# Sparse block attention and a gated feed-forward on one core: 64-query blocks against one 128-row tile of keys and summaries

## The chip, the core and the metric

The kernel runs on one core of one Trainium2 chip. The core has a matrix engine (PE, whose weight loads are listed apart as PEld), a vector engine (DVE), a scalar engine (ACT), GpSimd (POOL), and a sync engine (SP) that here only issues DMAs. They run side by side and wait for one another by semaphores. The metric is the device time of one execution in microseconds (us), lower is better. The kernel before takes 266.48 us, the median of three runs (266.11, 266.48, 267.84).

## What is computed

```python
batch, n_heads, seq, head_dim = (4, 8, 768, 64)      # q, k, v, float32
block, window = (32, 16)
k_sum = k.reshape(B, H, nb, block, D).max(axis=3)     # 24 summaries for each head
v_sum = v.reshape(B, H, nb, block, D).mean(axis=3)
scores_l = scale * q @ k^T, kept where |i - j| < window, else -1e9
scores_s = scale * q @ k_sum^T + log(block)
a = softmax(concat[scores_l, scores_s]);  x = a @ concat[v, v_sum]
# then for the 3072 tokens, d_model 512, d_ff 2048
h = x @ w_in
out = (h * clip(h + 3, 0, 6) / 6) @ w_out
```

A query sees 31 neighbouring keys at most and the 24 summaries of its head. Adding log(32) to a summary's score and taking the mean of v is the same as weighting its exponential by 32 in the row sum and taking the sum of v in the numerator; both kernels use this.

## The kernel before

**Units.** There are four batches and four head pairs `p` in each; a pair's two heads lie in partitions 0 to 63 and 64 to 127. Tokens are cut into eight tiles of 384 (`HALF`), two for each batch; tile `t` is batch `t // 2`.

**Attention of a pair.** `Tk` (L264) transposes k on PE, copies it out of PSUM into `kbd`, a block-diagonal tile with 64 keys of both heads in each of 12 steps, and takes the maximum over each 32 keys (`red`) into `kst`. `Tq` (L298) does the same with q into `qT`. `Sl` (L316) multiplies each 64-key block by the 94 queries that can see it (12 matmuls of 94 columns for a pair), takes the exponential on ACT (L324) and multiplies by a 0/1 band mask on DVE (L325). `Ss` (L327) makes the summary scores, for two pairs together: two matmuls of 384 columns for each half. `AV` (L348) makes one pair's half tile: the numerator `num` is one 384-column matmul with the summaries' values (L357) and seven 15- to 94-column matmuls over key blocks (L359); the row sum `den` is four matmuls with tiles of ones (L363, L366, L369 and L370, or L372 and L373). Then ACT takes the logarithm of `den` and the exponential of its negative (L375, L376), and DVE multiplies (L377) into `x`.

**Feed-forward.** `F1(t, ft)` (L382) is four 384-column matmuls (L389), a Relu on ACT (L392) and a combined minimum and product on DVE (L393) into `g`. `F2` (L395) is 512-column matmuls (L402), a copy on ACT (L406) and a store by SP (L408).

**Loads.** All but the stores and one small copy (L259) are issued by POOL, in program order. k and q of batches 0 and 1 are loaded as long runs (`RUN` = 8 rows of one partition) and transposed in 64-column pieces; those of batches 2 and 3 come in 256-byte rows (L111). Values go to the block-diagonal `vall` (L118); batch 0's come as float32 (`vf`, L127), are cast by ACT and DVE (`vcast`), and summed on PE by float32 matmuls (`vsum0`, L252). For batches 1 to 3 a second copy of v (`vr`, L134) is summed on DVE (`vsum`, L231 to L236).

**Order.** The start is written out by hand for PE, ACT and DVE (L151 to L448): attention of the first half of batch 0. After that a planner orders PE, ACT, DVE and SP; POOL stays in program order. The loop at the end runs `work_list` in slots: each entry is 16 slots of one F1 tile, one F2 tile or both, and `at_slot` puts attention steps into slots. The order is F1(0); F1(1) with F2(0); F2(1); F1(2); then F1(3) with F2(2) and so on, four F1 matmuls and three F2 matmuls in turn; last F2(7) alone. PSUM: `ps_h`, `ps_o` and `ps_s` have two buffers each, `ps_n` has one `num` and one `den`. The SBUF pool `gp` has three buffers, for `g` and for `vf`.

Of the kernel before, what the change touches and what calls it, by code (L numbers as in the profile page):

```python
# [16 lines left out]
D = 64  # L17
BLK = 32
KB = 64
HALO = 15  # L20
WIN = KB + 2 * HALO
HALF = 384
NLONG = 2
RUN = 8
PCS = 4
RP = 96
QCUT = 480
# [3 lines left out]
def kernel(  # L31
# [12 lines left out]
    NB = S // BLK  # L44
    NT = S // 128
    NK = S // KB
# [5 lines left out]
    RS = 4 * NB  # L52

    const = ctx.enter_context(tc.tile_pool(name="const", bufs=1))
    ld = ctx.enter_context(tc.tile_pool(name="ld", bufs=4))
    work = ctx.enter_context(tc.tile_pool(name="work", bufs=2))
    xp = ctx.enter_context(tc.tile_pool(name="xp", bufs=4))
# [11 lines left out]
    kbd = [const.tile([128, NK, 128], BF16, tag=f"kbd{p}", name=f"kbd{p}") for p in range(NP)]  # L69
    vall = const.tile([128, NP, NK, 128], BF16, tag="vbd", name="vbd")  # L70
    vbd = [vall[:, p] for p in range(NP)]
    qT = [const.tile([128, S + 2 * HALO + 2], BF16, tag=f"qT{p}", name=f"qT{p}") for p in range(NP)]
    at = [const.tile([128, NK, WIN], BF16, tag=f"at{p}", name=f"at{p}") for p in range(NP)]
    kst = [const.tile([128, RS], BF16, tag=f"kst{p}", name=f"kst{p}") for p in range(NP)]
    vst = [const.tile([RS, 2, D], BF16, tag=f"vst{p}", name=f"vst{p}") for p in range(NP)]
    w_in_sb = const.tile([128, NP, d_ff], BF16, tag="win", name="win")
    w_out_sb = const.tile([128, NFT, d_model], BF16, tag="wout", name="wout")


    kb_t, qb_t, vr_t, vf = {}, {}, {}, {}  # L80

    def load_k(b, p, n=1):

        if b < NLONG:
            t = ld.tile([RP, 2 * n, RUN, D], BF16, tag=f"kb{n}", name="kb", bufs=2)
            nc.gpsimd.dma_start(out=t[:], in_=k[b, 2 * p:2 * p + 2 * n].rearrange("h (p s) d -> p h s d", s=RUN))
        else:
            t = ld.tile([128, NT, 2, D], BF16, tag="kb", name="kb")
            load_natural(t, k, b, p)
        for i in range(n):  # L90
            kb_t[b, p + i] = t, i

    def load_q(b, p, n=1, part=None):

        if b < NLONG:
            lo, hi, r = cut(part)
            t = ld.tile([(hi - lo) // r, 2 * n, r, D], BF16, tag=f"qb{n}", name="qb", bufs=1 if n == 4 else 2)
            nc.gpsimd.dma_start(
                out=t[:], in_=q[b, 2 * p:2 * p + 2 * n, lo:hi].rearrange("h (p s) d -> p h s d", s=r))
        else:  # L100
            t = ld.tile([128, NT, 2, D], BF16, tag="qb", name="qb")
            load_natural(t, q, b, p)
        for i in range(n):
            qb_t[b, p + i, part] = t, i

    def cut(part):
        return {None: (0, S, RUN), 0: (0, QCUT, RUN // 2), 1: (QCUT, S, RUN // 2)}[part]

    def load_natural(t, src, b, p):
        for j in range(2):  # L110
            nc.gpsimd.dma_start(out=t[:, :, j], in_=src[b, 2 * p + j].rearrange("(s p) d -> p s d", p=128))  # L111

    def load_v(b, g, lo=0, hi=NK):

        for p in (2 * g, 2 * g + 1):
            for j in range(2):
                rows = slice(64 * j, 64 * j + 64)
                nc.gpsimd.dma_start(out=vall[rows, p, lo:hi, rows],  # L118
                                    in_=v[b, 2 * p + j].rearrange("(n k) d -> k n d", k=KB)[:, lo:hi])

    def load_vf(p):

        if not vf:
            t = gp.tile([128, NP, NK, D], F32, tag="g", name="vf")
            vf.update({i: t[:, i] for i in range(NP)})
        for j in range(2):
            nc.gpsimd.dma_start(out=vf[p][64 * j:64 * j + 64],  # L127
                                in_=v[0, 2 * p + j].rearrange("(n k) d -> k n d", k=KB))
# [416 lines left out]
```

## Time and profile before

| what | us |
|---|---|
| median of the runs | 266.48 |
| span of the profiled execution | 262.8 |
| median less span (launch and end, not in the span) | 3.7 |
| first F1 matmul | 34.85 |
| first matmul of F1(3), where F1 and F2 begin to alternate | 122.25 |
| last matmul ends | 258.8 |
| engine busy: PE, ACT, DVE, POOL | 238.0, 169.3, 154.2, 72.5 |

The span runs from the first to the last instruction of one execution under the profiler. An engine's busy time says how much of the span it had an instruction under way. A group row gives a line's operation, its tiles and shape, the count, its total and mean duration, and the idle time of its engine before it. A matmul's duration includes its latency, since matmuls overlap; the time that a stream of them takes is read from the starts of successive groups in the timeline.

### The profile page before, as it was taken

What the parts mean: (1) busy time and instruction counts of PE and PEld (TensorE: products, weight loads), DVE (VectorE), ACT (ScalarE), POOL (GpSimd) and SP (SyncE); (2) the same over time, 40 slices, a digit from 0 to 9 for tenths busy, and PEclk for the clock granted to TensorE, in tenths of its full rate; (3) what the DMA queues carried; (4) which work ended last, traced back from release to release, by engine and by line L of the source; (5) the groups of instructions that cost most, each with busy time, mean ns of one, the idle gap of its engine ahead of it and who ended that gap; (6) DMA issues with size and microseconds to landing.
All of it is one profiled execution on the core that took longest, in us unless ns stands there. A gap on an engine that the chain in (4) does not pass through costs nothing.

```text
span 262.8 us, 4842 instructions
## 1 busy us (share of the span) xinstructions
PE 238.0 (91%) x1848; PEld 135.9 (52%) x1872; DVE 154.2 (59%) x360; ACT 169.3 (64%) x327; POOL 72.5 (28%) x104
## 2 busy tenths in 40 slices
PE   0946899999899969999899999999999999999993
PEld 0215556644455636666455556566655555555541
DVE  3594556632889774998994566668534544444400
ACT  7665578842587867998586567757766555555410
POOL 8994000566273600796920310000000000000000
PEclk9995599999999999999999999999999999999999
DMA  3999994299999971899990551001011111101122
GB/s 111 178 155 201 206 206 76 37 204 209 203 255 118 180 80 44 58 130 187 185 145 19 54 70 44 36 7 40 2 40 40 42 40 40 40 2 41 40 82 80
DMA packets 57848, 25.80 MB, mean 98 GB/s; under 512 B 45281, under 2 KB 53217, under 8 KB 57825
## 3 DMA queue, kind: packets, MB, share of 16 engines
q0 software_dynamic: 54160, 19.14, 63.5%
q1 hardware_dynamic: 3664, 6.34, 6.5%
q8 instruction: 15, 0.25, 0.4%
q14 instruction: 9, 0.07, 0.1%
HBM read 31.98 MB, written 6.29 MB: 146 GB/s over the span
## 4 chain that ended last, share of the span: by engine, by line
PE 62%; DMA 11%; DVE 8%; ACT 7%; POOL 7%; issue 3%; ACTq 0%; POOLq 0%
PE op L402 24%; PE hp L389 24%; DMA vr<-in_v_dram 8%; POOL vbd L118 3%; PE num L359 2%; DMA vs<-vs 2%; PE sl L321 2%; POOL vf L127 2%; DVE g L393 2%; PE num L357 2%; PE ss L331 2%; ACT kbd L281 2%; PE den L363 1%; PE den L366 1%; DMA vf<-in_v_dram 1%
## 5 line engine op out<-in xcount | busy, mean ns | idle before, releaser
L389 PE MATMUL hp<-x,win 128*128 128x384 bf16 x512 | 104.1, 326 | 2.8 <-DVE g L393 2.4
L392 ACT ACTIVATE r<-hp,half_c 128x384 f32<-128x384 f32 x128 | 73.5, 580 | 45.8 <-PE hp L389 45.0
L402 PE MATMUL op<-wout,g 128*128 128x512 bf16 x360 | 96.2, 379 | 1.1 <-issue 0.2
L393 DVE SCALAR_TENSOR_TENSOR g<-r,hp 128x384 bf16<-128x384 f32 x128 | 69.6, 551 | 45.6 <-ACT r L392 45.4
L389 PEld LDWEIGHTS <-win 128*128 128x128 bf16 x512 | 47.3, 98 | 37.2 <-issue 6.0
L402 PEld LDWEIGHTS <-g 128*128 128x128 bf16 x384 | 36.8, 98 | 32.8 <-issue 0.5
L377 DVE TENSOR_TENSOR x<-num,lg 128x384 bf16<-128x384 f32 x32 | 17.7, 555 | 24.7 <-ACT lg L376 22.8
L118 POOL DMA_DIRECT2D vbd<-in_v_dram x24 | 18.2, 775 | 37.7 <-PE num L359 33.6
L375 ACT ACTIVATE lg<-den 128x384 f32<-128x384 f32 x32 | 15.7, 492 | 16.0 <-PE den L373 7.4
L324 ACT ACTIVATE at<-sl 128x376 bf16<-128x376 f32 (+2 forms) x48 | 22.4, 490 | 2.3 <-PE sl L321 2.3
L406 ACT COPY ot<-op 128x512 f32<-128x512 f32 x24 | 13.9, 583 | 8.9 <-PE op L402 8.8
L325 DVE TENSOR_TENSOR at<-at,mask 128x376 bf16<-128x376 bf16 (+2 forms) x48 | 16.2, 349 | 3.6 <-ACT at L324 3.4
L359 PEld LDWEIGHTS <-vbd 128*128 128x128 bf16 x224 | 13.8, 102 | 8.0 <-issue 4.5
L376 ACT ACTIVATE lg<-lg 128x384 f32<-128x384 f32 x32 | 16.8, 526 | 0.8
L321 PE MATMUL sl<-qT,kbd 128*128 128x94 bf16 x192 | 15.0, 214 | 1.9 <-ACT at L324 0.8
L321 PEld LDWEIGHTS <-kbd 128*128 128x128 bf16 x192 | 12.2, 102 | 7.7 <-issue 1.8
L359 PE MATMUL num<-at,vbd 128*128 128x94 bf16 (+2 forms) x224 | 15.0, 206 | 0.0
L111 POOL DMA_DIRECT2D qb<-in_q_dram x16 | 13.5, 861 | 4.8 <-DMA vr<-in_v_dram 4.8
L252 PE MATMUL vps<-vf,ind 128*8 128x384 f32 x16 | 7.5, 612 | 7.6 <-DMA vf<-in_v_dram 7.6
L111 POOL DMA_DIRECT2D kb<-in_k_dram x16 | 13.5, 865 | 0.0
L357 PE MATMUL num<-asum,vst 96*128 96x384 bf16 x32 | 11.0, 344 | 2.6 <-DVE x L377 2.2
L281 ACT COPY kbd<-tp 64x768 bf16<-64x768 bf16 x12 | 9.5, 792 | 5.2 <-PE tp L271 5.1
(82 smaller groups left out, 219.8 us busy)
## 6 DMA issues: line engine op xcount, KB each, us to landing
out_dram<-ot SPq DMA_DIRECT2D x24, 256.0 KB, 2.0
vr<-in_v_dram POOLq DMA_DIRECT2D x6, 768.0 KB, 7.7
vbd<-in_v_dram POOLq DMA_DIRECT2D x24, 96.0 KB, 3.9
win<-in_moe_w_in_dram POOLq DMA_DIRECT2D x4, 512.0 KB, 11.1
wout<-in_moe_w_out_dram POOLq DMA_DIRECT2D x4, 512.0 KB, 18.3
vf<-in_v_dram POOLq DMA_DIRECT2D x8, 192.0 KB, 3.7
kb<-in_k_dram POOLq DMA_DIRECT2D x16, 96.0 KB, 6.8
qb<-in_q_dram POOLq DMA_DIRECT2D x16, 96.0 KB, 6.4
```

The source lines that it names most:

```text
L111: nc.gpsimd.dma_start(out=t[:, :, j], in_=src[b, 2 * p + j].rearrange("(s p) d -> p s d", p=128))
L118: nc.gpsimd.dma_start(out=vall[rows, p, lo:hi, rows], in_=v[b, 2 * p + j].rearrange("(n k) d -> k n d", k=KB)[:, lo:hi])
L321: nc.tensor.matmul(sp[:, i * WIN:(i + 1) * WIN], kbd[p][:, t], qT[p][:, t * KB:t * KB + WIN], start=True, stop=True)
L324: nc.scalar.activation(a, sp[:, 0:n * WIN].rearrange("p (n c) -> p n c", c=WIN), AF.Exp, scale=scl)
L357: nc.tensor.matmul(num[:], vst[p][:].rearrange("p h d -> p (h d)"), asm[:], start=True, stop=False)
L359: nc.tensor.matmul(num[:, lo:hi], vbd[p][:, t], a[:, t, off:off + hi - lo], start=False, stop=(i == len(bl) - 1))
L376: nc.scalar.activation(lg[:], lg[:], AF.Exp, scale=-1.0)
L377: nc.vector.tensor_tensor(xt[s][:, p], num[:], lg[:], op=ALU.mult)
L389: nc.tensor.matmul(hp[:], w_in_sb[:, kt, ft * 128:(ft + 1) * 128], xt[t][:, kt], start=(kt == 0), stop=(kt == NP - 1))
L392: nc.scalar.activation(r[:], hp[:], AF.Relu, bias=half_c[:], scale=1.0 / 6.0)
L393: nc.vector.scalar_tensor_tensor(gt[t][:, ft], r[:], 1.0, hp[:], op0=ALU.min, op1=ALU.mult)
L402: nc.tensor.matmul(op[:], gt[t][:, ft, ts * 128:(ts + 1) * 128], w_out_sb[:, ft], start=(ft == 0), stop=(ft == NFT - 1))
```

## The change

- **Scores.** `KB`, `HALO` and the block-diagonal tiles go. `kx` holds for each of 12 query blocks of 64 a 128-row tile: 96 adjacent keys (16 before, the block, 16 after), the 24 summaries, and 8 rows of zero. `qx` holds the 64 queries of both heads beside each other, with zeros in the other head's partitions. `Sc` makes 64 queries of both heads in one 128-column matmul. The neighbours' edge columns and the summaries are placed into `kx` by three DVE copies (L267 to L269); `Ss`, `kst`, `asum` go.
- **Mask.** In batches 0 and 1 (`MASK_ON_PE`) PE first adds a bias tile through the identity (L301, 512 or 256 columns); in batches 2 and 3 DVE multiplies by a mask after the exponential.
- **Values.** `va[i]` holds for each pair and block three 64-column groups: head A's values and sums, a middle group, head B's. In batches 0 and 1 the middle is zero, and `num` takes 12 matmuls of 64 columns and `den` two of 384 with ones. In batches 2 and 3 (`DEN_IN_VALUES`) the middle is 1 (32 in the summary rows), so that each 64-column matmul gives one head's numerator and row sum; there is no separate `den`.
- **Loads of v.** Windows of 96 rows for each block come by overlapping reads: batches 0 and 1 as float32 (`load_vf`), cast on POOL (`cast_v`); batches 2 and 3 straight to bf16, eight DMAs. Sums of batch 0: 48 float32 matmuls of 128 columns (`sum_v`); of batches 1 to 3: additions on POOL (`vsum`), spread to the 12 blocks by SP DMAs.
- **Loads of k and q.** Long runs for batches 0 to 2 (`NLONG` = 3); the first half of batch 0's q is 384 rows.
- **Order.** The second half of batch 0 moves beside F2(0); `work_list` runs F1(0), F2(0), F1(1), F2(1), F1(2) each alone, and F1(3) with F2(2) from slot 80 on (slot 64 before); all slots are new. SP is in the hand-written order of the start.

```diff
 def Tk(b, p):
...
+        nc.scalar.copy(o.rearrange("p t (c s) -> p t c s", s=RUN),
+                       tp[:].rearrange("p (s t c) -> p t c s", s=RUN, t=NQ))
...
+    nc.vector.tensor_copy(kx[p][:, :, R_SUM:R_SUM + NB], red[:].unsqueeze(1).to_broadcast([128, NQ, NB]))
+    nc.vector.tensor_copy(kx[p][:, 1:, 0:EDGE], kx[p][:, 0:NQ - 1, QB:QB + EDGE])
+    nc.vector.tensor_copy(kx[p][:, 0:NQ - 1, EDGE + QB:R_SUM], kx[p][:, 1:, EDGE:2 * EDGE])
...
+def Sc(b, p, lo, hi):
+    n = hi - lo
+    sp = ps_s.tile([128, 4, 2, QB], F32, tag="s", name="sp")
...
+    if on_pe:
+        nc.tensor.matmul(sp[:, 0:n], ident[:], maskb[:, m0:m0 + n].unsqueeze(2).to_broadcast([128, n, 2, QB]),
+                         start=True, stop=False)
+    for i in range(n):
+        t = lo + i
+        nc.tensor.matmul(sp[:, i], kx[p][:, t], qx[p][:, t], start=not on_pe, stop=not on_pe or i == n - 1)
+    a = at[p][:, lo:hi]
+    nc.scalar.activation(a, sp[:, 0:n], AF.Exp, scale=scl)
+    if not on_pe:
+        nc.vector.tensor_tensor(a, a, mask[:, m0:m0 + n].unsqueeze(2).to_broadcast([128, n, 2, QB]), op=ALU.mult)
...
 def AV(b, p, half):
...
+    if b in DEN_IN_VALUES:
+        for j, o in enumerate((num, den)):
+            for i in range(NH):
+                t = half * NH + i
+                w = va[b % 2][:, p, t].rearrange("p j d -> p (j d)")
+                nc.tensor.matmul(o[:, i * QB:(i + 1) * QB], w[:, j * D:j * D + 128], a[:, t, j],
+                                 start=True, stop=True)
+        nc.scalar.activation(lg[0:64], num[64:128], AF.Ln)
+        nc.scalar.activation(lg[64:128], den[0:64], AF.Ln)
+        nc.scalar.activation(lg[:], lg[:], AF.Exp, scale=-1.0)
+        nc.vector.tensor_tensor(xt[s][0:64, p], num[0:64], lg[0:64], op=ALU.mult)
+        nc.vector.tensor_tensor(xt[s][64:128, p], den[64:128], lg[64:128], op=ALU.mult)
+        return
+    for i in range(NH):
+        t = half * NH + i
+        w = va[b % 2][:, p, t].rearrange("p j d -> p (j d)")
+        for j in range(2):
+            nc.tensor.matmul(num[:, i * QB:(i + 1) * QB], w[:, j * D:j * D + 128], a[:, t, j],
+                             start=(i == 0 and j == 0), stop=(i == NH - 1 and j == 1))
+    w = ones[:].rearrange("p j d -> p (j d)")
+    for j in range(2):
+        nc.tensor.matmul(den[:].rearrange("p (t c) -> p t c", c=QB), w[:, j * D:j * D + 128],
+                         a[:, half * NH:(half + 1) * NH, j], start=(j == 0), stop=(j == 1))
...
 def vsum(b, g):
...
+    while n > 1:
+        n //= 2
+        o = r[:, 0:n] if n > 1 else vs[:]
+        nc.gpsimd.tensor_tensor(out=o, in0=r[:, 0:n], in1=r[:, n:2 * n], op=ALU.add)
+    for i in range(4):
+        h = 4 * g + i
+        nc.sync.dma_start(out=va[b % 2][R_SUM:R_SUM + NB, h // 2, :, 2 * (h % 2)],
+                          in_=vs[i * NB:(i + 1) * NB].to_broadcast([NB, NQ, D]))
...
+def cast_v(b, p, lo, hi):
+    t = vf_t[b, p // 2][0:R_SUM, 2 * (p % 2):2 * (p % 2) + 2, lo:hi]
+    nc.gpsimd.tensor_copy(va[b % 2][0:R_SUM, p, lo:hi, 0:3:2].rearrange("r t j d -> r j t d"), t)
...
+def sum_v(p):
+    for t in range(NQ):
+        nc.tensor.matmul(sums[R_SUM:, 2 * p:2 * p + 2], ind[:, 31 - 2 * t:63 - 2 * t],
+                         vf_t[0, p // 2][0:R_SUM, 2 * (p % 2):2 * (p % 2) + 2, t],
+                         start=(t == 0), stop=(t == NQ - 1))
+
+def put_sums(p, lo, hi):
+    o = va[0][R_SUM:, p, lo:hi, 0:3:2].rearrange("r t j d -> r j t d")
+    nc.gpsimd.tensor_copy(o, vs0[R_SUM:, 2 * p:2 * p + 2].unsqueeze(2).to_broadcast([32, 2, hi - lo, D]))
...
+scores0(0)
+S_first(0)
+sum_v(0)
+sum_v(1)
+scores0(1)
+S_first(1)
+sum_v(2)
+sum_v(3)
+scores0(2)
+nc.scalar.copy(vs0[R_SUM:], sums[R_SUM:])
+for i in range(2):
+    cast_v(0, 2 * i, 0, NH)
+    cast_v(0, 2 * i + 1, 0, NH)
+    load_w_in(2 * i)
+    load_w_in(2 * i + 1)
+for p in range(NP):
+    put_sums(p, 0, NH)
+S_first(2)
+scores0(3)
+AV(0, 0, 0)
+S_first(3)
+for p in range(1, NP):
+    AV(0, p, 0)
+load("q", 0, 0, 4, 1)
+for c in range(2):
+    load_w_out(c)
+for p in range(NP):
+    cast_v(0, p, NH, NQ)
+    put_sums(p, NH, NQ)
+for c in range(2, 4):
+    load_w_out(c)
+for p in range(NP):
+    nc.vector.memset(words(va[1][:, p, :, 1]), 0.0)
+    for j in (0, 2):
+        nc.vector.memset(words(va[1][R_SUM:, p, :, j]), 0.0)
...
+for g in range(2):
+    vf_t[1, g] = gp.tile([128, 4, NQ, D], F32, tag="g", name="vf")
+    load_vf(1, 2 * g, 2)
+
+def rest_of_1():
+    load("q", 1, 2, 2)
+    load_vrows(1, 1)
+    vsum(1, 0)
+    for p in range(2):
+        cast_v(1, p, 0, NQ)
+    vsum(1, 1)
+    for p in range(2, 4):
+        cast_v(1, p, 0, NQ)
...
+def loads(b):
+    load_vrows(b, 0)
+    load_vrows(b, 1)
+    weights_between(b % 2)
+    for h in range(H):
+        load_v(b, h)
+    vsum(b, 0)
+    vsum(b, 1)
...
+at_slot(22, rest_of_1)
+for b, s0, s1 in ((2, 48, 56), (3, 71, 81)):
+    at_slot(s0, lambda b=b: load_kq(b, 0))
+    at_slot(s1, lambda b=b: (load_kq(b, 2), loads(b)))
+attention(1, 42, 4, lambda i: (56, 58, 61, 63, 65, 68, 71, 74)[i])
 for b in range(2, B):
-    base = 48 + 32 * (b - 2)
+    base = 64 + 32 * (b - 2)
...
-work_list = ([(0, None), (1, 0), (None, 1), (2, None)] + [(t, t - 1) for t in range(3, NTILE)]
+work_list = ([(0, None), (None, 0), (1, None), (None, 1), (2, None)] + [(t, t - 1) for t in range(3, NTILE)]
```

Line numbers of the kernel after, where the prediction uses them, are those of its own file: `Tk` L247, `Tq` L271, `Sc` L295, `AV` L313, `F1` L353, `F2` L365, `sum_v` L384.

## The prediction, made before the changed kernel ran

> **What bounds the kernel now.** I read the page's busy shares first, then busy time by stage, then the timeline of PE for what a stream of matmuls costs.
>
> ```profile
> 34.85:122.25 87.40, 82.46 (x762) 48.80 (x768) 62.20 (x139) 65.23 (x132) 40.01 (x53) 1.00 1.16 140
> 122.25:258.80 136.55, 134.32 (x901) 76.11 (x914) 72.92 (x150) 80.84 (x156) 11.37 (x15) 1.00 0.35 53
> ```
>
> The rows are stretches of the span with its length and then the busy time of PE, PEld, DVE, ACT and POOL: PE is busy 134.3 of 136.6 us in the late stage and 82.5 of 87.4 in the early one, the others about half to three quarters. PE sets the time, so the price of a matmul stream decides. The timeline of PE, with start, length and line:
>
> ```profile
> 48.22 0.20 PE L372 MATMUL den<-at,obd 128*128 128x75 bf16 x1
> 48.26 0.20 PE L373 MATMUL den<-at,obd 128*128 128x90 bf16 x1
> ...
> 103.48 0.50 PE L305 MATMUL tp<-ident,qb 128*128 128x128 bf16 x6
> 103.82 0.33 PE L389 MATMUL hp<-x,win 128*128 128x384 bf16 x1
> ...
> 14.37 1.45 PE L252 MATMUL vps<-vf,ind 128*8 128x384 f32 x4 [1.06 <-DMA vf<-in_v_dram]
> ```
>
> Starts give the price: 75 columns with fresh 128x128 weights take 0.04 us (48.22 to 48.26), six 128-column ones 0.34 us, 0.056 each; the F1 pieces of the chain give 0.1625 us for 384 columns (four in 0.65), F2 0.216 for 512. Float32: two records make one 384-column matmul, four records take 1.45, so 0.72 us each.
>
> I split the span in four and count the matmuls of each stage in the built order, at these prices. Start, to the first F1: 34.85. Early stage, F1(0) to F1(2) and their F2: 77.0 priced against 87.4 measured, 10.4 lost in waits. Late stage from F1(3): 134.5 priced, 136.5 measured, 2.0 lost. Tail after PE: 4.0. Sum 262.8, the span; the median of the runs is 3.7 above it.
>
> **The change on PE.** Row sums and values: an AV costs 0.1625 + 7 x 0.039 + 0.1625 + 0.17 + 2 x 0.04 = 0.85 us. After, in batches 0 and 1, 12 matmuls of 64 columns and two of 384; in batches 2 and 3 the 12 alone. No row has 64 columns with fresh weights: 75 columns take 0.03 to 0.04, so I take 0.0335, with ends 0.027 (columns in proportion to 384 in 0.1625) and 0.056 (nothing gained under 128). So 0.73 and 0.40 us. Scores: 12 x 0.042 for `Sl` and, for each pair, 0.33 for `Ss`, 0.82 us; after, 12 x 0.056 = 0.67, plus 0.65 for the mask's 1536 columns in batches 0 and 1. Batch 2's transposes go from 12 x 0.056 to 32 x 0.03, 0.3 more for a pair. Counted over the order: late stage 134.5 to 127.7, **6.8 saved**; early stage 77.0 to 78.5, since all the mask matmuls lie there, **1.5 added**.
>
> A rule speaks against these prices. The Trainium skill ("TensorE: Matmul & The Clock Gate", Back-to-back issue gap) puts a sustained stream of weight load and 128-column matmul at about 81 ns each; the rows above have 56 and 34. By the page the 168 late and early score matmuls would cost 4.2 us more, an estimate; the measurement decides and I leave it out.
>
> **The start, on PE and around it.** It sums batch 0's values by 48 float32 matmuls of 128 columns; by the 384-column row a third of 0.72, 0.24 each, 11.5 us for 5.8 before (ends: 10 by columns alone, 23 at the half clock that the page's PEclk row shows in slices 4 and 5). They stand in order between the first scores and the later pairs. k of pair 0 now goes first and lands about 4.5 us (before, values issued at 1.33 landed at 4.8). A pair's chain is then: transposes 0.5, ACT copy 0.8, DVE maximum 0.96, three small copies about 0.2 each, a q copy 0.5: 3.5 us (the copies have no row; a 96x64 add took 0.22). With values at 1.2 us for 768 packets (two casts of pair 0 start 1.1 us apart) and half as many packets again, the four pairs' values land at about 9, 13, 18 and 21 us. PE: first scores 9.7, sums of pairs 0 and 1 to 15.5, pair 1 to 19.3, sums of 2 and 3 to 25.1, pair 2 to 28.9, pair 3 to 33.2, AV to 36.3. So the first F1 is at about **36.5**, 1.6 later; ends 34 and 42.
>
> Two things are late right after it. `gp` has three buffers: batch 1's `vf` are allotted ahead of `g`, so F1(0)'s first product waits for POOL's last cast from the second `vf` (POOL: sums by 30.7, three DMA issues of 0.8, seven casts and copies; at about 0.8 for 768 elements, from 0.31 for a 256-element memset and 0.6 for a 256-element select: 39; at 1.6, 45). And twelve memsets on DVE stand ahead of that product: 12 x 0.45 (L199: two in 0.88) = 5.4 us after the last AV product at 38, so 43.5. PE runs four F1 groups ahead on its PSUM buffers, then stands; F1(0) ends at 51.9 for 46.9 without it: **5.0 us lost**. Of the 10.4 lost before, I drop what has a cause that goes: half clock at F1's start 1.0, the wait for batch 1's k at 62 to 68 1.4, the wait of AV for DVE at 94 to 96 2.6 (DVE gives its `vsum`, 3 us for two pairs, to POOL); and 1.0 that F1(0) had. The other 4.4 stay. Early loss 9.4.
>
> **What moves to the other engines.** ACT takes both k copies, and three activations in place of two for an AV in batches 2 and 3: busy 169 to about 173 us (16 more logarithms at 0.49 and more q copies at 0.8, fewer k copies, casts and zero copies), below PE everywhere but slots 64 to 79, where F1(2), batch 2's transposes and five AV need 20 of ACT and DVE against 18.4 of PE; that 2 is within the 4.4. POOL gets additions: no POOL row adds two tensors; the DVE's add to 2.97 us for a group (two halves, 1984 elements), and POOL's selects at 1.6 to 2.4 ns an element give 3.2 to 4.7; I take 4.7. Its order blocks: `rest_of_1` ends near 82 us, then two k and q loads, 8 memsets, 8 value loads at 0.95 and a `vsum`: batch 2's sums are in `va` at about 109; their first AV, slot 78, comes at about 118. Nine us of cover. The SP copies of batch 1's sums stand ahead of all stores in SP's queue; three output buffers cover that until F2(1) writes its first at about 85, when they are out.
>
> POOL and DVE also meet. Rows of the start:
>
> ```profile
> 8.45 0.26 POOL L167 TENSOR_SCALAR_AFFINE_SELECT mask<-mask 64x94 bf16<-64x94 bf16 x1
> 8.77 0.47 POOL L169 TENSOR_SCALAR_AFFINE_SELECT mask<-mask 64x94 bf16<-64x94 bf16 x1
> 9.62 0.26 POOL L169 TENSOR_SCALAR_AFFINE_SELECT mask<-mask 64x94 bf16<-64x94 bf16 x1
> ...
> 8.48 0.63 DVE L243 CAST vbd<-vf 64x768 bf16<-64x768 f32 x1 [0.57 <-DMA vf<-in_v_dram]
> ...
> 15.89 0.49 DVE L243 CAST vbd<-vf 64x768 bf16<-64x768 f32 x1
> ```
>
> The select beside the DVE's cast took 0.47 for 0.26, the cast 0.63 for 0.49: a meeting costs about 0.2. Some 60 DVE copies and mask products can meet some 50 us of POOL work; a fifth of them at 0.2 is 2 us of DVE, mostly where DVE has room, so I book none. The Trainium skill ("SBUF — State Buffer", Who interferes with whom) says more: the pair of ports is held for a whole instruction, and the other engine waits it out. By that each meeting with a 2.3 us addition (its estimate for 1024 elements, from "GPSIMD Engine Reference", Elementwise) costs DVE up to 2.3, half of that on average, and twelve of them some 14 us of DVE. The rows show the sign and not that size.
>
> **Sum.** 36.5 + 78.5 + 9.4 + 127.7 + 2.0 + 4.0 = 258.1 for the span, against 262.8; with 3.7, **261.8 us**, against 266.5. Its own range is 257 to 265: 1.0 and 1.2 for the 64-column price's lower end in the early and late stage, the 4.4 gone or kept, 2 us of the start.
>
> **Rivals.**
> - *The start is later.* Half clock or slow casts put the first F1 at 42 and not 36.5: 263.6 + 3.7 = 267.3, range 265 to 270. For it: PEclk fell to 5 tenths when PE waited 3.6 us at 17 to 20 us; against: the float32 sums keep PE in work.
> - *POOL becomes the bound (slower).* Its queue has 27 us of work (two `vsum` of batch 1, four casts of 2, memsets, a `vsum` of batch 2) ahead of batch 2's first AV and 9 us of cover. From 1.33 times my price PE stands at slot 78; at 1.75 times by 27 x 0.75 - 9 = 11 us: 272.8; range 268 to 280. It must lose more than 3.6 us of the gain to be over before. For it: the one-engine order and no row for the add; against: the late stage gives time, and batch 3 has twice the room.
> - *Weights pace the short matmuls (slower).* If 64 columns cost 0.056, the 150 early and 186 late ones cost 7.6 more: 269.4. The 75-column rows speak against.
> - *The waits go.* The hand order removes the 4.4, and F1(0)'s 5.0 halves: 254.9; range 251 to 257.
>
> **Chances.** Forecast 0.48, later start 0.20, POOL 0.12, weights 0.04, waits gone 0.16. About 1% is what a measurement of this kernel tells from no change: faster is below 263.8, slower above 269.2. Faster: 0.16 and 0.41 of the 0.48, 0.57. Slower: 0.11 of POOL, 0.03 of weights and 0.06 of the late start, 0.20. Same: 0.23. The range for eight in ten, 254 to 270, takes in most of the waits rival and the late start and leaves POOL's upper part out.
>
> **What would show it.** Right: the first F1 near 36.5; F1(0) stopped by DVE memsets (its product waiting for POOL or following L435 and L437); 64-column starts 0.03 apart; F1(3) at about 124; PE close to 136 us from there to its end less 7. Wrong: F1(3) later than 131; a wait of L329 for SP copies or POOL; 64-column starts over 0.045 apart; masks (L309) or edge copies (L268, L269) that last over 1 us beside L150.

## The result: 281.56 us, 6% slower, and the profile after

The changed kernel takes 281.56 us (median of three runs, 280.68 to 282.03) against 266.48: a ratio of 1.060, 95% interval 1.050 to 1.071. The profiled execution has a span of 280.0 us, where the prediction's sum made it 258.1.

The page of the changed kernel: busy time of each engine, then the busy tenths of two engines and the granted clock in 40 slices of 7 us, then the chain of waits by engine.

```profile
PE 245.9 (88%) x2036; PEld 146.2 (52%) x2060; DVE 156.0 (56%) x328; ACT 174.0 (62%) x326; POOL 121.0 (43%) x151
...
PE   1787478399999997995999999999899999999994
...
POOL 7963399400797108999969999000000000000000
PEclk9997958689999999999799999999999999999999
...
PE 60%; DVE 19%; ACT 14%; issue 5%; POOL 2%; ACTq 0%; DVEq 0%; POOLq 0%
```

POOL has 121 us of work for 72.5, up to slice 25. PE has holes in the start, in slice 8 (3 tenths, 49 to 56 us) and in slice 19 (5 tenths, 126 to 133), and after each the clock is low (5 to 8 tenths in slices 6 to 9, 7 in slice 20). DVE has 19% of the chain, for 8% before. By stages (length, then busy time of PE, PEld, DVE, ACT and POOL, clock, DMA share, GB/s): to the first F1, F1(0) to F1(2), from F1(3).

```profile
0.00:44.33 44.33, 29.05 (x279) 23.28 (x280) 15.51 (x54) 14.29 (x27) 30.97 (x50) 0.85 0.95 154
44.33:142.40 98.07, 87.39 (x871) 51.54 (x875) 62.72 (x120) 68.36 (x129) 58.94 (x65) 0.95 0.95 146
142.40:276.45 134.05, 129.45 (x896) 71.36 (x909) 77.77 (x155) 90.74 (x170) 31.13 (x37) 1.00 0.38 63
```

Against the prediction's terms: the start 44.3 for 36.5 (+7.8), the early stage 98.1 for 78.5 + 9.4 (+10.2), the late one 134.05 for 127.7 + 2.0 (+4.4), the tail 3.55 for 4.0. Together 21.9 us, the whole error. Three places show how. First the start, PE's timeline: start, length, what, and in brackets how long it stood and for whom.

```profile
10.33 8.67 PE L386 MATMUL sums<-vf,ind 96*32 96x128 f32 x48
...
22.97 7.09 PE L386 MATMUL sums<-vf,ind 96*32 96x128 f32 x48
...
34.79 0.58 PE L305 MATMUL sp<-qx,kx 128*128 128x128 bf16 x4 [3.77 <-DVE qx L291]
```

A float32 matmul makes two records, so 24 took 8.67 and then 7.09 us: 0.36 and 0.30 each, where the prediction had 0.24. These means hide two rates. In the first group the records start 0.21 us apart up to 17.0 and 0.11 apart from there on; in the second 0.11 apart, then 0.21 from 23.8 to 27.2, where the granted clock is 0.50, then 0.11 again. So a matmul takes 0.22 at the faster rate and 0.43 at the slower. For the second group that is the clock; before 17.0 the profile shows a clock of 1.00, so that the clock was low there too is argued and not shown.

The wait at 34.79 is longer than pair 1's 2.48 at the same line. DVE's timeline shows why: L267 to L269 of pair 1, then of pair 2, in which POOL copies sums (L392, from POOL's timeline: 32.40 to 35.63, 0.8 each).

```profile
21.33 0.23 DVE L267 COPY kx<-red 128x288 bf16<-128x288 bf16 x1
21.48 0.20 DVE L268 COPY kx<-kx 128x176 bf16<-128x176 bf16 x1
21.60 0.19 DVE L269 COPY kx<-kx 128x176 bf16<-128x176 bf16 x1
...
32.54 0.83 DVE L268 COPY kx<-kx 128x176 bf16<-128x176 bf16 x1
33.29 0.85 DVE L269 COPY kx<-kx 128x176 bf16<-128x176 bf16 x1
```

The same instruction takes 0.83 for 0.20. The second place is F1(2), at 127 to 132 us, timeline of all engines:

```profile
127.02 0.94 DVE L264 TENSOR_REDUCE red<-tpk 128x24 bf16<-128x768 bf16 x1
127.24 5.01 POOL L150 TENSOR_TENSOR vr<-vr 96x1024 f32<-96x1024 f32 x4
127.89 1.76 DVE L268 COPY kx<-kx 128x176 bf16<-128x176 bf16 x1
129.57 0.21 DVE L267 COPY kx<-red 128x288 bf16<-128x288 bf16 x1
129.71 1.28 DVE L269 COPY kx<-kx 128x176 bf16<-128x176 bf16 x1
130.91 0.53 DVE L363 SCALAR_TENSOR_TENSOR g<-r,hp 128x384 bf16<-128x384 f32 x1
...
131.50 0.48 PE L359 MATMUL hp<-x,win 128*128 128x384 bf16 x2 [2.59 <-DVE g L363]
```

POOL's first addition of 1024 elements takes 2.35 us (its mean by shape), so it ends at 129.59; L268 ends at 129.65. The second (512 elements, 1.27) ends at about 130.9; L269 ends at 130.99. Each copy stands until the addition that it met is over. Behind them stands F1's product, behind that a PSUM buffer, and PE waits 2.59 us; from 133.1 to 136.5 its clock is 0.50. The maximum (L264), which reads PSUM, keeps its 0.94.

The third is F1(0), timelines of DVE and PE:

```profile
47.06 0.38 DVE L435 MEMSET va<- 128x384 f32 x1
...
51.90 0.78 DVE L437 MEMSET va<- 32x384 f32 x2
...
53.33 3.04 PE L359 MATMUL hp<-x,win 128*128 128x384 bf16 x9 [4.95 <-DVE g L363]
```

PE waits 4.95 us at 53.33 for `g`, which stands behind the memsets L435 and L437 from 47.06 to 52.7, as predicted. What was not: the clock is 0.50 from 51.1 to 58.0 us. PE works 4.6 us of that stretch, so about 2.3 us are lost by it, an estimate that takes the rate as proportional to the clock.

### The profile page after: what moved, and what is told of

Its sections match the earlier page's. It is cut to its first block, busy times and chain, and to the rows that moved or that the text cites. A ratio compares the mean times of both kernels' runs of the same rounds, so it can differ in the third digit from the quotient of the medians.

```text
span 280.0 us, 5284 instructions
## 1 busy us (share of the span) xinstructions
PE 245.9 (88%) x2036; PEld 146.2 (52%) x2060; DVE 156.0 (56%) x328; ACT 174.0 (62%) x326; POOL 121.0 (43%) x151
## 4 chain that ended last, share of the span: by engine, by line
PE 60%; DVE 19%; ACT 14%; issue 5%; POOL 2%; ACTq 0%; DVEq 0%; POOLq 0%
PE op L371 22%; PE hp L359 21%; PE sums L386 6%; DVE g L363 3%; PE sp L305 3%; DVE red L264 3%; ACT at L307 3%; DVE qx L291 3%; ACT r L362 2%; DVE kx L269 2%; ACT kx L256 2%; PE num L341 2%; PE sp L301 2%; ACT lg L331 2%; ACT lg L332 2%
## 5 line engine op out<-in xcount | busy, mean ns | idle before, releaser
L307 ACT ACTIVATE at<-sp 128x512 bf16<-128x512 f32 (+1 forms) x52 | 27.6, 563 | 20.1 <-PE sp L305 19.9
L150 POOL TENSOR_TENSOR vr<-vr 96x1024 f32<-96x1024 f32 (+3 forms) x24 | 28.9, 1204 | 2.1 <-DMA vr<-in_v_dram 0.5
L305 PE MATMUL sp<-qx,kx 128*128 128x128 bf16 x192 | 19.1, 228 | 11.2 <-DVE qx L291 11.1
L264 DVE TENSOR_REDUCE red<-tpk 128x24 bf16<-128x768 bf16 x12 | 11.5, 956 | 31.2 <-ACT kx L256 30.9
L305 PEld LDWEIGHTS <-kx 128*128 128x128 bf16 x192 | 15.1, 102 | 21.3 <-issue 13.3
L386 PE MATMUL sums<-vf,ind 96*32 96x128 f32 x96 | 15.8, 346 | 0.0
L291 DVE COPY qx<-tpq 64x384 bf16<-64x384 bf16 (+1 forms) x16 | 12.2, 761 | 4.5 <-ACT qx L291 4.1
L386 PEld LDWEIGHTS sums<-vf,ind 96*32 96x32 f32 x96 | 13.5, 143 | 2.0 <-issue 0.2
L123 POOL DMA_DIRECT2D va<-in_v_dram x17 | 14.4, 875 | 0.0
L132 POOL CAST va<-vf 96x768 bf16<-96x768 f32 (+1 forms) x12 | 12.3, 1039 | 3.3 <-DMA vf<-in_v_dram 3.1
L309 DVE TENSOR_TENSOR at<-at,mask 128x512 bf16<-128x512 bf16 x24 | 10.8, 462 | 4.4 <-ACT at L307 4.2
## 6 DMA issues: line engine op xcount, KB each, us to landing
vf<-in_v_dram POOLq DMA_DIRECT2D x2, 1152.0 KB, 23.3
```

The lines of the kernel that those rows point to most:

```text
L123: nc.gpsimd.dma_start(out=o[r0:r1, c0:c1], in_=src(r0, r1, c0, c1))
L150: nc.gpsimd.tensor_tensor(out=o, in0=r[:, 0:n], in1=r[:, n:2 * n], op=ALU.add)
L264: nc.vector.tensor_reduce(red[:], tp[:].rearrange("p (s n c) -> p n s c", s=RUN, n=NB), axis=AX.XY, op=ALU.max)
L291: copy(o.rearrange("p t (c s) -> p t c s", s=r), tp[rows, 0:n].rearrange("p (s t c) -> p t c s", s=r, t=nt))
L305: nc.tensor.matmul(sp[:, i], kx[p][:, t], qx[p][:, t], start=not on_pe, stop=not on_pe or i == n - 1)
L307: nc.scalar.activation(a, sp[:, 0:n], AF.Exp, scale=scl)
```

## The experiments

All edits are to the kernel after unless they say so. The table gives the time, the kernel before beside it, and three marks from ACT's Relu instructions: when the first one of F1(0) starts, from there to the first of F1(3), and from there to the start of the last. Between profiles of kernels with the same start the first mark spreads from 45.9 to 47.5, so of a time from one execution 1.6 us may be that; the other two marks don't hold it. Each time is of one execution, but for the first two rows and the last three. The last mark spreads from 120.9 to 121.3 in the four kernels with the late stage of the kernel after; how far the middle one spreads isn't known, so a microsecond of it is not much.

| kernel | us | before | F1(0) at | to F1(3) | to the end |
|---|---|---|---|---|---|
| before | 266.48 | | 37.2 | 86.5 | 124.1 |
| after | 281.56 | 266.48 | 47.4 | 97.0 | 121.0 |
| memsets_early | 278.15 | 266.16 | 46.5 | 94.0 | 121.0 |
| sums_sixth | 275.45 | 266.16 | 38.9 | 99.2 | 120.9 |
| one_add | 276.06 | 266.16 | 46.7 | 92.3 | 120.8 |
| den_apart | 275.33 | 266.16 | 45.9 | 94.0 | 119.2 |
| edges_on_act | 279.49 | 266.54 | 48.6 | 93.4 | 121.0 |
| adds_on_dve | 297.95 | 266.54 | 46.1 | 109.0 | 126.5 |
| start_bf16 | 274.48 | 266.54 | 39.9 | 96.9 | 121.3 |
| four_undone | 288.10 | 266.54 | 39.4 | 105.8 | 126.6 |
| adds_on_dve_late | 295.83 | 263.85 | 47.5 | 107.2 | 124.8 |
| three_undone | 265.84 | 263.85 | 40.6 | 89.5 | 119.4 |
| three_edges | 262.82 | 263.85 | 39.7 | 88.0 | 118.8 |
| three_adds_late | 289.73 | 263.85 | 40.4 | 105.9 | 127.1 |
| den_apart_memsets | 279.73 | 266.89 | 46.6 | 96.1 | 120.5 |
| ordered_start | 259.85 | 266.89 | 33.9 | 90.9 | 118.8 |
| ordered_mask0 | 266.68 | 266.89 | 34.7 | 96.9 | 118.8 |
| batch1_bf16 | 252.72 | 265.01 | 31.4 | 85.8 | 118.8 |
| batch1_mask_all | 256.74 | 265.01 | 32.3 | 85.3 | 122.1 |
| batch1_row_sums | 256.95 | 266.67 | 32.6 | 86.6 | 121.0 |

### One part at a time

**memsets_early.**

```diff
     scores0(0)
     S_first(0)
+    for p in range(NP):
+        nc.vector.memset(words(va[1][:, p, :, 1]), 0.0)
+        for j in (0, 2):
+            nc.vector.memset(words(va[1][R_SUM:, p, :, j]), 0.0)
```

(and taken out at the end of the start)

> The twelve memsets of va[1] go to just after the first scores of pair 0, where DVE is idle (9 to 20 us). Theory A, DVE holds F1(0)'s first product and the half clock that follows is part of the same stop: the loss in F1(0) falls from 8.1 us to 1 to 3, no PE stop over 1 us at 45 to 55, time 275 to 277 for 281.6. Rival, the third buffer of gp: the product waits for POOL's last cast of batch 0 all the same and the loss stays at 6 or more, time 280 to 282. Rival, given back: F1(0) ends 5 us earlier, but F1(1) or the attention of batch 1 then waits for its loads, and F1(3) begins less than 2 us earlier than 142.4.

The wait of 4.95 is gone, and F1(1)'s first Relu comes 7.7 us earlier (74.0 for 81.7). But F1(2)'s comes only 3.8 earlier, F1(3)'s 3.9. The timeline of all engines at F1(1):

```profile
81.49 5.02 POOL L150 TENSOR_TENSOR vr<-vr 96x1024 f32<-96x1024 f32 x4 [8.08 <-DMA vr<-in_v_dram]
82.36 1.55 DVE L268 COPY kx<-kx 128x176 bf16<-128x176 bf16 x1
...
83.97 1.28 DVE L269 COPY kx<-kx 128x176 bf16<-128x176 bf16 x1
...
85.75 0.32 PE L359 MATMUL hp<-x,win 128*128 128x384 bf16 x1 [1.66 <-DVE g L363]
```

POOL's additions start when their rows land, at 81.5 as in the kernel after (81.65). There they met only products that read PSUM; now, with PE further on, they meet the k copies of batch 1, which last 1.55 and 1.28, and the clock is 0.50 from 86.7 to 90.1. The memsets were the cause of F1(0)'s stop, and the meeting took half of the gain.

**sums_sixth.**

```diff
-        for t in range(NQ):
+        for t in (0, NQ - 1):
             nc.tensor.matmul(sums[R_SUM:, 2 * p:2 * p + 2], ...
```

> Leaves out ten of the twelve float32 matmuls of each pair's sums (8 for 48 in all; batch 0's summaries are then sums of two blocks alone). Theory B, the float32 matmuls are the path of the start until the values' landing takes over: the second group can't begin before the last values land (23.3 us), so it ends at 24.5 for 30.1, and the first F1 comes 5 to 6 us earlier, at 38.5 to 39.5; time 275 to 277. If the landing is no floor the first F1 is at 32 to 34, time 270 to 272. Rival, the start is bound by the copies of ACT and DVE and by POOL's casts and weight loads: the first F1 is less than 2 us earlier, time 280 or more.

The first Relu comes 8.5 us earlier, more than the expectation left for the landing: the last sums start at 21.7, after a wait of 0.8 for values, and not at 23.3. The sums are on the path of the start. 2.2 us go back in the early stage.

**start_bf16.**

```diff
-    ind = const.tile([RP, 2 * BLK], F32, tag="ind", name="ind")
+    ind = const.tile([RP, 2 * BLK], BF16, tag="ind", name="ind")
...
-    load_vf(0, 0, 1)            # and pairs 1 to 3
+    load_v(0, 0)
+    load_v(0, 1)
...
         for t in range(NQ):
             nc.tensor.matmul(sums[R_SUM:, 2 * p:2 * p + 2], ind[:, 31 - 2 * t:63 - 2 * t],
-                             vf_t[0, p // 2][0:R_SUM, 2 * (p % 2):2 * (p % 2) + 2, t],
+                             va[0][0:R_SUM, p, t, 0:3:2],
...
-        cast_v(0, 2 * i, 0, NH)     # and all other casts of batch 0
```

> Batch 0's values come by DMAs that write bf16 straight into va, as those of batches 2 and 3 do; the sums are 48 bf16 matmuls from there, and POOL's eight casts of batch 0 go. Theory B: the sums cost 48 x 0.056 = 2.7 us for 15.7, and the start is then held by the landing of values (23 us) and pairs 2 and 3 behind it: first relu at 37 to 40 for 47.4, and F1(0)'s product no longer waits for a cast but for the memsets: time 271 to 275. Rival, the DMAs that convert land later (batches 2 and 3 issue one in 0.87 us for each head): first relu at 44 or later, time 279 or more.

7.5 us in the start, all kept. The matmuls took 1.46 us for 12 and 2.74 for 24 (PE's timeline), 0.11 to 0.12 each and not 0.056, as the float32 ones took twice their time at first. The page's clock row has 9 tenths there, so a low clock is again argued and not shown.

**one_add.**

```diff
-        n = BLK
+        n = 2
         vs = work.tile([RS, 1, D], BF16, tag="vs", name="vs")
```

> Leaves out four of the five additions of each vsum (the sums of blocks are then of two keys): POOL loses about 26 of its 121 us of work. Theory C, the additions on POOL hold DVE's copies and masks and PE stands for that: the stretch 104 to 142 loses about 6 us less, L268, L269 and L309 have means near those alone (0.19, 0.20, 0.41 us), F1(3) begins at 136 to 137, time 274 to 276. Rival, a drip of ACT and DVE work that has nothing to do with POOL: less than 2 us, time 280 or more, and the means stay. Rival, the landing of loads that POOL issues late: the gain shows as waits for DMA that go, and not in the means.

4.7 us between F1(0) and F1(3), 0.2 after. L268's mean falls from 381 to 256 ns and L309's from 462 to 422, but L269's only from 474 to 388, since one of its copies stands 1.57 us at 106.6, where POOL issues loads and then writes the memsets between the values: it ends at 108.18, with the first memset (108.13). The copies at 126 to 134 take 0.20 to 0.60. DMA issues alone do this too: in the kernel after three copies of 0.51, 0.64 and 0.62 us (at 120.09, 138.00 and 146.27) stand beside nothing else on POOL and end at 120.59, 138.64 and 146.89, where an issue ends at 120.53, 138.61 and 146.87.

**edges_on_act.**

```diff
-        nc.vector.tensor_copy(kx[p][:, 1:, 0:EDGE], kx[p][:, 0:NQ - 1, QB:QB + EDGE])
+        nc.scalar.copy(kx[p][:, 1:, 0:EDGE], kx[p][:, 0:NQ - 1, QB:QB + EDGE])
```

(L267 and L269 alike)

> The three small copies into kx (L267 to L269) go from DVE to ACT, POOL's additions stay. Theory C in its narrow form, POOL holds DVE only in copies from SBUF to SBUF: the copies now take 0.2 to 0.5 us each on ACT beside the additions too, F1(3)'s first relu comes 3 to 5 us earlier than 144.5, and the start gains 2 to 3 us (POOL's put_sums held pair 2's copies by 6). Time 275 to 278. Rival, POOL's lateness or ACT's load: ACT has 10 us more, no gain or a loss, time 281 to 284. What the mask products (L309) lose stays in both.

3.6 us come out of the early stage, although POOL does all its additions: ACT's timeline, two copies while POOL issues loads and two beside an addition,

```profile
119.34 0.33 ACT L268 COPY kx<-kx 128x176 bf16<-128x176 bf16 x1
119.56 0.34 ACT L269 COPY kx<-kx 128x176 bf16<-128x176 bf16 x1
...
127.31 0.37 ACT L268 COPY kx<-kx 128x176 bf16<-128x176 bf16 x1
127.54 0.38 ACT L269 COPY kx<-kx 128x176 bf16<-128x176 bf16 x1
```

So it is the meeting that costs, not the additions' lateness; nor is it DVE's load, since one_add leaves the copies on DVE and gains 4.7 there. The start gained nothing (48.6): ACT has the chain of each pair there, and the copies take 0.33 to 0.47 on it for 0.2. The mask products on DVE still stand beside the additions (one of 1.02 at 125.8).

**adds_on_dve.**

```diff
-            nc.gpsimd.tensor_tensor(out=o, in0=r[:, 0:n], in1=r[:, n:2 * n], op=ALU.add)
+            nc.vector.tensor_tensor(out=o, in0=r[:, 0:n], in1=r[:, n:2 * n], op=ALU.add)
```

> All additions of vsum go from POOL to DVE, as before the change. The run with one addition left shows what their absence gives, 5.6 us. Theory C, they cost by holding DVE and not by their own work: on DVE each group takes about 3 us and 24 in all, DVE stays under 70% and the time is 277 to 279. Rival, DVE has no room for them: the matmuls of F1 wait for g, time 282 or more.

16 us slower than after, but for neither reason: DVE stood 19.7 us in four waits for the rows to land, the longest 10.9, and PE 18.7 us in one behind it. The additions themselves are short on DVE (1.22 us for 1024 elements, 2.35 on POOL).

**adds_on_dve_late.** The same with `vsum` taken out of `rest_of_1` and `loads`, and

```diff
+    for b, g, s in ((1, 0, 49.2), (1, 1, 53.2), (2, 0, 66.2), (2, 1, 71.2), (3, 0, 92.2), (3, 1, 94.2)):
+        at_slot(s, lambda b=b, g=g: vsum(b, g))
```

> The additions on DVE again, but each group is put in order only where its rows have landed (slots 49, 53, 66, 71, 92, 94), since the run with them on DVE at their old places had DVE stand 19.7 us for those rows. Theory C: without POOL's additions the copies and masks of the early stage are short again, DVE works 24 us more beside, and the time is 276 to 279. Rival, DVE has no room: 282 or more, with waits of F1 for g behind the additions.

The edit didn't do what the expectation says of it. Outside the start DVE's order is the planner's, and it put the first group ahead of F1(0)'s products all the same; DVE's timeline:

```profile
62.61 2.72 DVE L150 TENSOR_TENSOR vr<-vr 96x1024 f32<-96x1024 f32 x4 [9.95 <-DMA vr<-in_v_dram]
...
65.55 1.95 DVE L363 SCALAR_TENSOR_TENSOR g<-r,hp 128x384 bf16<-128x384 f32 x4
```

Whether DVE has room for the additions once their rows are there was not settled by these runs.

**den_apart and den_apart_memsets.** Row sums of batches 2 and 3 by matmuls with ones. The first also takes out the call of `weights_between`, and with it POOL's memsets; the second keeps them, with zeros (L472 alike).

```diff
-DEN_IN_VALUES = (2, 3)
+DEN_IN_VALUES = ()
...
-            nc.gpsimd.memset(va[i][0:R_SUM, p, :, 1], 1.0)
+            nc.gpsimd.memset(va[i][0:R_SUM, p, :, 1], 0.0)
```

> Batches 2 and 3 take the row sums by two matmuls with ones as batches 0 and 1 do, and POOL loses the memsets between the values. By the prices of the matmul streams PE has 16 x 0.33 = 5.3 us more work from slot 78 on. Theory D, the two-part logarithms and products of an AV cost the late stage its 4.4 us of new waits: those go, and the time is 281 to 284. Rival, the late waits come from short stages in general: the time is the full price above, 286 to 288.

> Row sums apart in batches 2 and 3, as in the run that gained 6.3 us, but POOL keeps the sixteen memsets between the values (they write 0 here, so that the outputs stay the same). Theory D, the three activations and two products of an AV cost: the late stage loses nothing again, F1(3) to F1(7)'s last relu takes 119 to 120 us, time 275 to 278. Rival, POOL's memsets (12 us) cost, by holding DVE or by making POOL late: the gain goes, 280 to 283, with the difference between F1(2) and F1(3).

The first gained 6.2 us, with 5.3 us more for PE by the prices: outside both expectations. From F1(0) on it gains 4.8 (213.2 for 218.0), the second 1.5 (216.5). So both causes are there: the memsets 3.3 us (2.0 early, 1.3 late), and the AV's extra steps 1.5 beyond the 5.3 that they were to save. With the memsets the copy of 1.57 us is there again, at 106.58, and the late part is one wait of 0.97 us at 173.81: POOL's last additions start at 168.75, for 163.56 in the first run, and meet batch 3's copies (0.85 and 0.74 for 0.20). Busy time from F1(3) to the last Relu (the columns as above), first after, then den_apart_memsets:

```profile
144.50:265.50 121.00, 116.77 (x823) 65.49 (x838) 75.72 (x151) 86.36 (x164) 29.39 (x35) 1.00 0.40 63
```

```profile
142.70:263.20 120.50, 118.48 (x871) 68.51 (x886) 67.85 (x135) 79.55 (x149) 30.46 (x37) 1.00 0.41 64
```

DVE has 7.9 us more and ACT 6.8 in the kernel after, and neither is busy over 72%. The AV's steps cost by their place: F1 with F2 has two PSUM buffers, and three activations (0.49, 0.48, 0.52) and two products of 0.55 stand in one piece between two Relus. PE's timeline of one AV in the kernel after:

```profile
161.54 0.34 PE L329 MATMUL num<-at,va 128*128 128x64 bf16 x6
161.85 0.33 PE L329 MATMUL den<-at,va 128*128 128x64 bf16 x6
162.34 0.81 PE L359 MATMUL hp<-x,win 128*128 128x384 bf16 x4 [0.16 <-DVE g L363]
```

Six matmuls take 0.17, so the second six start 0.14 late, and F1, which could follow them at 162.02, is 0.32 later still: 0.46 us lost, more than the 0.33 that the AV saves. This is one of the two worst of 16; in four others F1 comes 0.19 to 0.26 late. Elsewhere the loss comes at a later F1: PE's longest wait of the stage, 0.51 us at 156.87, is for a `g` behind the two products (155.09 to 156.23). By the difference of the runs it is 6.8 us for 16 AVs, 0.43 each. In den_apart the list of PE's waits is empty in this stage.

### Parts together

**four_undone** (memsets early, start in bf16, row sums apart without memsets, additions on DVE), **three_undone** (without the last), **three_edges** (three and the edges on ACT), **three_adds_late** (three and the additions as in adds_on_dve_late).

> Four parts together: memsets early, start in bf16, additions on DVE, row sums apart in batches 2 and 3. If the causes stand side by side the gains add up to about 4 + 8 + 4 + 6 = 22 us: 259 to 262, below the kernel before. If they overlap (the same work is late behind each, as a half of the memsets' gain was given back) it is 264 to 270.

> Three parts together, POOL keeps the additions: memsets early, start in bf16 by converting DMAs, row sums apart in batches 2 and 3. One by one they gave 3.9 (of 7.7, the rest went back where POOL's additions met the first k copies of batch 1), 7.1 and 6.3 us. Side by side: 264 to 266; if the meeting with the additions takes back the half again on top: 267 to 270.

> The same three and the small kx copies on ACT, which alone gave 2.1 us (4.1 between F1(1) and F1(3), with 1.2 lost in the start). Theory C: what the additions took back goes, 2 to 4 us below the run with three. Rival, ACT is now the one that is late: no gain.

> The same three and the additions on DVE at late places. Theory C: 3 to 5 us below the run with three, 260 to 263. Rival, DVE has no room: at or above the run with three.

Three parts give 15.7 us of the 16.7 that they gave one by one (3.4, 7.1 and 6.2), so their causes stand nearly side by side, as far as rounds can be compared (the kernel before took 263.85 in this one). The edges on ACT give 3.0 more, and with these four parts undone the kernel is level with the one before. The two with additions on DVE miss every expectation: they have their wait for the rows again (24.5 us in each).

**ordered_start**, on three_edges:

```diff
     scores0(0)
+    scores0(1)
     S_first(0)
-    sum_v(0)
-    sum_v(1)
-    scores0(1)
+    scores0(2)
     S_first(1)
-    sum_v(2)
-    sum_v(3)
-    scores0(2)
+    scores0(3)
+    sum_v(0)
+    sum_v(1)
+    S_first(2)
+    S_first(3)
+    sum_v(2)
+    sum_v(3)
```

(the memsets behind; values of pairs 1 to 3 issued after all k and q; batch 0's edges on DVE)

> On top of the run with three parts undone and the edges on ACT: the start in another order. k and q of all pairs are issued ahead of the values of pairs 1 to 3, the transposes of the next pair stand ahead of the scores of this one (PE waited 3.3 us for each pair's copies), sums after them, and batch 0's edges are on DVE again. If the pair chains are what holds the start: first relu at 30 to 34 for 39.7, time 255 to 259. Rival, the loads of batch 1 or the weights are then late: half or more given back by F1(3), time 260 to 263.

The start gains 5.8 us, 2.9 are given back. DVE's and ACT's waits name where:

```profile
DVE g L361 <- POOL va L132: 6.4, 1, 6.4
```

```profile
ACT ot L373 <- DMA out_dram<-ot: 3.2, 1, 3.2
```

The first is `gp`'s third buffer: `g` of F1(1) waits for POOL's cast out of batch 1's `vf`. The second is SP's queue: stores stand behind the copies of batch 1's second sums, whose rows were issued at 51.8 and landed at 74.

**ordered_mask0** (`MASK_ON_PE = (0,)` on the ordered start) and, also on the ordered start, **batch1_bf16**:

```diff
-    for g in range(2):
-        vf_t[1, g] = gp.tile([128, 4, NQ, D], F32, tag="g", name="vf")
-        load_vf(1, 2 * g, 2)
+    load_vrows(1, 1)
+    for h in range(H):
+        load_v(1, h)
```

(and `rest_of_1` without casts and that load); on it **batch1_mask_all** (`MASK_ON_PE = (0, 1, 2, 3)`) and **batch1_row_sums** (`DEN_IN_VALUES = (2, 3)` and the memsets again).

> The same as the run with the ordered start, with batch 1's mask as products on DVE in place of additions on TensorE. PE has 4 x 0.65 = 2.6 us less by its prices, DVE 12 x 0.43 = 5.2 more, where POOL's additions stand beside. If PE sets the early stage: 1 to 2.5 us faster; rival, the masks meet POOL's additions: 0 to 3 us slower.

> On top of the ordered start: batch 1's values too come by converting DMAs straight into va, and the rows for its sums are loaded ahead of them. In the run with the ordered start DVE stood 6.4 us for POOL's casts of batch 1 (PE 3.0), and an output copy on ACT waited 3.2 us for stores that stand in SP's queue behind the copies of batch 1's second sums (PE 2.6). If these are what was given back: 5 us faster, 254 to 256. Rival, the loads themselves are late (22 us from issue to landing for the second rows): 258 to 261.

> The same with the masks of batches 2 and 3 added on TensorE too: by the prices PE has 8 x 0.65 = 5.2 us more, DVE 12 x 0.46 = 11 less in 24 products. Moving batch 1's mask to DVE had cost 6.8 us. If DVE's masks hold PE in F1(2) and later as they did there, 1 to 3 us faster than the run beside it; if PE sets the late stage, as its waits of under 2 us there say, 3 to 5 us slower.

> The run with batch 1 in bf16, with the change's row sums out of the value products in batches 2 and 3 put back, POOL's memsets with them. In the kernel after, taking this part out gave 6.3 us, 1.9 of them with the memsets left in. Theory: it costs ACT and DVE steps and POOL time wherever it stands, so 2 to 6 us slower, 255 to 259. Rival, it only cost because DVE and POOL were late from the start on, and PE's 5.3 us count once they are not: 1 to 4 us faster, 249 to 252.

With batch 1's mask as DVE products the kernel is 6.8 us slower, more than either expectation, although PE has 2.6 less by its prices. But that isn't the price of the masks. ACT's waits have the queue of stores again, longer:

```profile
ACT ot L373 <- DMA out_dram<-ot: 6.1, 1, 6.1
```

Behind it PE stands 6.1 us at 91.33, for 2.6 before, and the clock is 0.50 from 89.4 to 96.2. Six products that stand beside POOL's additions and cast last 0.84 to 1.85 for 0.42. What the masks cost by themselves, and why the stores came later, this run doesn't show. In batches 2 and 3 mask matmuls cost 4.0 (batch1_mask_all), near PE's price of 5.2.

batch1_bf16 gains 7.1 us, 5.1 of them in the early stage, as the first theory says, and 2.5 in the start, which it doesn't. It takes 252.72 us, a ratio to the kernel before of 0.953 (interval 0.948 to 0.959); batch1_mask_all has 0.969 (0.963 to 0.975), batch1_row_sums 0.968 (0.959 to 0.976). The row sums cost some 4 us there too: 2.2 late, 0.8 early, the rest in the start's spread. The page of batch1_bf16:

```profile
PE   1196799999999999899999999999999999999994
...
PEclk9999999999999999999999999999999999999999
```

No hole after slice 5, and no slice of the clock under 9 tenths.

## Why the prediction was wrong

The sum was short by 7.8 us in the start, 10.2 in the early stage and 4.4 in the late one. No rival's range holds 281.56. Two of the prediction's own signs of being wrong came: F1(3) at 142.4, later than 131, and copies of over 1 us beside L150.

**The start (+7.8).** The step "by the 384-column row a third of 0.72, 0.24 each" is mis-sized: 0.36 and 0.30, 4.0 us more. Its row was one of the fast rate. The first group of the same line in the profile before has eight records, four matmuls of 1.15 us each:

```profile
6.03 4.61 PE L252 MATMUL vps<-vf,ind 128*8 128x384 f32 x8 [6.03 <-DMA vf<-in_v_dram]
```

In the kernel after 0.22 at the fast rate is near the 0.24, but about half of the matmuls ran at 0.43. The end of 23 us "at the half clock" had been written down and then left at the lower side, because "the float32 sums keep PE in work"; they did, and the first 6.7 us still ran at the slower rate. The pair chain was right without POOL (pair 1: 4.0 us for 3.8) and 1.9 short for pair 2, 1.3 of it in the two copies that POOL's copies of sums held. First scores +0.6, pair 3 and the AVs +1.0. The rival "the start is later" had the direction and stopped at 42.

**F1(0) (5.0 booked).** The mechanism was right, and memsets_early shows it: 6.8 us less from F1(0) to F1(1). What was left out is the low clock that goes with such a stop, and that the time that PE stands hides something: 3.9 came back at once as a meeting with POOL.

**Meetings of POOL and DVE (booked at none).** This is the step whose mechanism failed: "a meeting costs about 0.2". Its rows had 0.26 us instructions on POOL, and a meeting costs up to the length of POOL's instruction. L267 to L269 and L309 lasted 29.0 us in the kernel after; at 0.23, 0.20, 0.19 and 0.41 alone it would be 19.8, so 9.2 us of DVE, not 2. Fourteen of these 72 instructions lost nearly all of it, about as many as the twelve that the prediction counted, at 0.65 each. Five stood beside additions (4.1 us), four beside POOL's copies and a cast in the start (2.0), one beside DMA issues and a memset (1.4) and four beside DMA issues alone (1.5). "Mostly where DVE has room" failed too: from 125 to 131 us, in F1(2), DVE is busy all 6.0 us. Without the additions the early stage was 4.7 us shorter.

The rule that the prediction set aside (the Trainium skill, "SBUF — State Buffer", Who interferes with whom: the engine that comes second waits out the whole instruction of the other) was right, and the 1.76 us copy shows it. The section adds that a reduction never contends and that ACT never waits. The trace agrees with both (0.94 beside the additions, 0.37 for 0.33), but this reduction reads PSUM, so it is no test of one that reads SBUF. The estimate from the rule, 14 us for twelve meetings with an addition, was too high for the additions, 4.1 in five; that POOL's copies, memsets and DMA issues hold DVE as well was in neither.

**Row sums out of the value products.** PE's saving was counted, ACT's and DVE's added steps only against their total load ("below PE everywhere but slots 64 to 79"). In the kernel after the part costs 4.8 us, 3.3 of them the memsets; the rest is the saving of 5.3 more than taken back. In the late stage, where 5.3 less was booked, it was 1.8 more, some 7 us apart: that covers the late +4.4 and the 2.0 of waits that the sum had kept, which den_apart doesn't have. The prediction had met it only as "that 2 is within the 4.4".

**Right.** 64 columns cost 0.029 us (six in 0.17), so "weights pace the short matmuls" is off, and the lower end of the price would have been nearer (of the prediction's "56 and 34" no row has the 34; the one for 75 columns has 40). The 128-column score matmuls start 0.056 apart, so the 4.2 us were rightly left out. POOL's group of additions took 5.4 to 5.8 us for 4.7, and PE never stood for POOL at slot 78: "POOL becomes the bound" named the engine, not the way.

**Open.** That DVE could take the additions if they were put where their rows have landed was not shown, nor whether the mask matmuls of batches 0 and 1 (5.2 us booked) are worth their price there. The new order of the work was never undone by itself. Between the causes of the early stage the split depends on order, since one part's gain moves the others' meetings. What the low clock alone costs was estimated and not measured.

## What to carry to other kernels

Price a step moved to GpSimd not only by its own length: look which copies and products from SBUF to SBUF stand on VectorE in that stretch, and let each that it can meet last until GpSimd's instruction ends, DMA issues on GpSimd included; put such copies on ScalarE, or GpSimd's work where VectorE reads PSUM. A saving on the bound engine that adds steps between two evictions counts only as far as the PSUM buffers reach, whatever the shares of busy time say. An edit that removes a stop lets later work arrive earlier, so ask what it meets there. And take a price from every row of its kind: a mean or a single row can hide two rates.

## What the runs showed of the hardware

- A VectorE copy of 0.20 us lasted 1.76 beside a GpSimd addition of 2.35 us, 0.83 beside its 0.8 us copies, and 0.37 for 0.33 when it ran on ScalarE.
- In three places a VectorE copy of 0.20 to 0.24 us lasted 0.51 to 0.64 beside a DMA issue of GpSimd and ended 0.02 to 0.06 us after it.
- The granted clock of TensorE was 0.50 from 51.1 to 58.0 us around a stop of 4.95 us that ended at 53.33, and from 133.1 to 136.5 after one of 2.59 us that ended at 131.50. In batch1_bf16 the mean clock was 0.998, for 0.957 after and 0.973 before.
- 96x128 float32 matmuls cost 0.22 us each, and 0.43 where the clock was 0.50 and in the first 6.7 us of the stream; bf16 ones of the same shape 0.11 to 0.12 in the same place.
- The addition of 1024 float32 elements took 2.35 us on GpSimd and 1.22 on VectorE.
